# Second mixture: the first expert's plain results weighed inside the additions of the second expert, and one slot product moved by two slots

## The chip, the core and the metric

One core of a Trainium2 chip runs the whole program as a single launch. The metric is the time of one execution on the device, in microseconds (us). Five engines share the work: TensorE (PE in the profile, its weight loads PEld), VectorE (DVE), ScalarE (ACT), GpSimd (POOL) and SyncE (SP), which here issues the transfers.

## The reference, cut to what matters

Three layers follow each other: an attention with a memory term, a mixture of experts over slots, and a second mixture. Only the third is touched. It gets x (2304 rows, 512 columns) and eight experts with weights of 512 x 1024 and 1024 x 512:

```python
logits = x @ w_gate
P = np.exp(logits - logits.max())
for _ in range(8):
    P /= P.sum(1, keepdims=True) + 1e-09
    P /= P.sum(0, keepdims=True) + 1e-09
    P *= N / E
for e in range(E):
    out += P[:, e:e+1] * (np.maximum(x @ w1[e], 0.0) @ w2[e])
```

The eight rounds on P are called the balancing below. P is not known before they have ended.

## The kernel before, in words

**The grid.** The second mixture is a list of 72 units: eight experts times nine row blocks `u` of 256 rows, expert by expert. Unit 0 is expert 0 with u = 0, unit 9 is expert 1 with u = 0, and so on. A unit multiplies hidden values (256 x 1024) with one expert's second weights (1024 x 512) and adds the result to accumulators that stay in SBUF: `accA`, `accB` and `accD`, which hold the four 128 x 256 blocks of each row block and one intermediate sum.

**Two kinds of units.** Units 0 to 5 (`RAW = 6`) run while the balancing is still under way. They multiply plainly (`plain`, L1336) and `store` their result unweighed on ScalarE. From unit 6 on, P is known and lies already in the hidden values, and a unit uses seven block products instead of eight (`product`, L1369 to L1371), in the order p5, p1, p7, p6, p2, p3, p4. Each product ends in PSUM, and `collect` adds it to an accumulator: on ScalarE as a copy where the accumulator is new (L1383), on VectorE as an addition otherwise (L1385).

**Slots.** A unit has seven slots, and slot s = 7 * unit + k. In each slot the engines' instruction lists get one product, or seven plain matmuls, and the side steps that a table `side` holds for that slot, in the order in which they were entered. The order on TensorE, VectorE, ScalarE and GpSimd is exactly that of the code.

**Preparing the next unit.** While a unit multiplies, its successor's hidden values are made. `layer1` (L1052) is TensorE's first layer for the next unit, in slot 1 of a product unit: eight matmuls into two PSUM banks. `hidden` then spreads work over slots 2 to 6 and slot 0 of the next unit: ScalarE takes relu and the high parts (L1072, L1082), VectorE sums and low parts out of PSUM (L1076, L1089), GpSimd the low parts of the sums (L1093). The last one on VectorE is `a22l` (L1089). After it the two banks are free for the next `layer1`.

**Side steps.** The next expert's weights are summed (`w_sum`, L960) and split into high and low parts (`w_hi` on ScalarE, L963, `w_lo` mostly on GpSimd, L969). For expert 1 the steps of T1, T2 and T4 stand in slots 29 to 51. `scale_c`, `turn_c` and `store_c` put P into the small matrix that `layer1` reads, in units 6 to 10 for expert 1 and in the same place of each later expert. `prepare_a` (L999) multiplies the slots with an expert's first weights into the one PSUM bank `aux`, `split_a` splits that (L1008, L1010), and `move_a` has SyncE copy it to its place. `sum_columns` (L1203, tile `pcs`) uses the same bank `aux` between `balance_rows` (L1189 to L1197) and `balance_columns` (L1207 to L1210), in slots 9 + 3n, 10 + 3n and 11 + 3n.

**Settling.** Units 0 to 5 left their results unweighed, so `settle` (L1279) multiplies the four blocks of row block u by column 0 of P, one 128 x 256 block per slot, in slots 3 to 6 of unit 6 + u. That is 24 instructions on VectorE, in units 6 to 11.

Of the kernel before, what the change touches and what calls it, by code (L numbers as in the profile page):

```python
# [12 lines left out]
ALU = mybir.AluOpType  # L13
# [8 lines left out]
def infini_attention_soft_moe_sinkhorn_moe(  # L22
# [15 lines left out]
    nc = tc.nc  # L38
# [73 lines left out]
    with ExitStack() as actx:  # L112
        def pool(nm, bufs=1):
# [13 lines left out]
            out=maskw[:, 3 * P :], in_=maskw[:, 3 * P :], compare_op=ALU.is_ge,  # L127
# [6 lines left out]
        for j in range(2):  # L134
            sl = maskt[64 * j : 64 * j + 64]
            nc.gpsimd.affine_select(
                out=sl, in_=sl, compare_op=ALU.is_ge,
# [6 lines left out]
        for i in range(QTB):  # L144
            pr = []
            for nm, w in (("qz", 3 * TAIL), ("qx", 2 * TAIL)):
                t = e2.tile([P, w], F32R, name=f"{nm}{i}")
# [5 lines left out]
        for i in range(2):  # L153
            t = ep[i].tile([P, 2, S], F32R, name=f"klz{i}")
# [75 lines left out]
        for c0, c1 in ((0, 2 * P), (2 * P, S)):  # L230
# [14 lines left out]
            out=gB[:, 1, :], in0=gB[:, 0, :], scalar1=-1.0, scalar2=1.0,  # L245
            op0=ALU.mult, op1=ALU.add,
# [427 lines left out]
        def at(p, n, f, *args):  # L674

            fill.setdefault(3 * NT * p + n, []).append((f, args))
# [84 lines left out]
    with bctx:  # L761
# [57 lines left out]
        for g in range(E // 4):  # L819
# [3 lines left out]
            for n in range(FF // 512):  # L823
# [3 lines left out]
                for c in range(KD):  # L827
                    for j in range(4):
                        e = SPE * (4 * g + j)
# [54 lines left out]
    CW = DM // 2  # L884
# [4 lines left out]
    RAW = 6  # L889
# [77 lines left out]
    def w_lo(e, nm, i, g):  # L967
# [12 lines left out]
        out=sel.rearrange("p j c -> p (j c)"), in0=ones[:, 0:1].to_broadcast([P, 640]),  # L980
        scalar1=0.0, scalar2=None, op0=ALU.mult,
# [59 lines left out]
    accA = mB.tile([P, NU, DM], F32, name="accA")  # L1041
    accB = mB.tile([P, NU, DM], F32, name="accB")
    accD = mB.tile([P, NU, CW], F32, name="accD")
# [83 lines left out]
    Pr = mB.tile([P, NTT, E], F32, name="Pr")  # L1127
# [120 lines left out]
    def beside(s, f, *args):  # L1248
        side.setdefault(s, []).append((f, args))
# [11 lines left out]
    def both(t):  # L1261
        return t.rearrange("p (o c) -> p o c", o=1).to_broadcast([P, 2, CW])

    def halves(t):
        return t.rearrange("p (o c) -> p o c", o=2)

    def add_u(u, g):

        A, B_, D_ = accA[:, u], accB[:, u], accD[:, u]
        eng(g[0]).tensor_tensor(  # L1270
            out=halves(B_), in0=halves(B_), in1=both(A[:, 0:CW]), op=ALU.add
        )
        eng(g[1]).tensor_tensor(out=D_, in0=D_, in1=A[:, 0:CW], op=ALU.add)

    def settle(u, i):

        A, B_, D_ = accA[:, u], accB[:, u], accD[:, u]
        t, T = ((A[:, CW:], 0), (B_[:, 0:CW], 0), (B_[:, CW:], 1), (D_, 1))[i]
        nc.vector.tensor_scalar(  # L1279
            out=t, in0=t, scalar1=Pr[:, 2 * u + T, 0:1], scalar2=None, op0=ALU.mult  # L1280
        )

    def at(u, k, f, *args):
        beside(7 * u + k, f, *args)

    def c_steps(v, e, u0, u1):
        at(v, 1, scale_c, e, u0, u1)
        at(v, 2, turn_c, e, u0, u1)
        at(v, 3, store_c, e, u0, u1)
# [15 lines left out]
    for e in range(1, E):  # L1305
        v = NU * (e - 1)
        for i in range(5):
            c_steps(v + 6 + i, e, 2 * i, min(2 * i + 2, NU))
        at(v, 0, load_w1, e, e % 2)
        at(v + 3 * (e == 1), 4, load_raw, e)  # L1310
        at(v + 1, 3, prepare_a, e)
        at(v + 1, 4, split_a, e)
        at(v + 1, 5, move_a, e)
        for i in range(2):
            for n, nm in enumerate(("T1", "T2", "T4")):

                s = 29 + 4 * (3 * i + n) if e == 1 else 7 * (v + 2 + 3 * i + n) + 1
                beside(s, w_sum, e, nm, i, "P")
                beside(s + 2 - (e == 1), w_hi, e, nm, i)
                beside(s + 3 - (e == 1), w_lo, e, nm, i, "P")  # L1320
            at(v + 6 + i, 2, w_sum, e, "T3", i, "P")
        for nm, k in (("B11", 2), ("T3", 4), ("B21", 6), ("B22", 8)):
            for i in range(2):
                at(v + 8, k + i, w_hi, e, nm, i)
                at(v + 8, k + i + (nm[0] == "B" and nm[1] == "2"), w_lo, e, nm, i, "D" if nm == "B22" and i else "P")
    for u in range(RAW):
        for i in range(4):
            at(6 + u, 3 + i, settle, u, i)


    def plain(g, k):
# [42 lines left out]
    def collect(g, k, y):  # L1374
        e, u = units[g]
        nm = ORDER[k]

        A, B_, D_ = accA[:, u], accB[:, u], accD[:, u]
        new, end = e == 0, e == E - 1

        def put(acc, y, new=new):
            if new:
                nc.scalar.activation(out=acc, in_=y, func=AF.Copy)  # L1383
            else:
                nc.vector.tensor_tensor(out=acc, in0=acc, in1=y, op=ALU.add)  # L1385

        def send(i, c, t):
            r0 = P * (2 * u + i)
            nc.sync.dma_start(out[r0 : r0 + P, CW * c : CW * c + CW], t)

        if nm == "p5":
            put(halves(B_), both(y))
        elif nm == "p1" and e == 1 and u < RAW:
            put(A[:, 0:CW], y, True)
            put(A[:, CW:], y)
        elif nm == "p1":
            put(halves(A), both(y))
        elif nm == "p7":
            put(D_, y)
        elif nm == "p2":  # L1400
            put(A, Y[g, "y3"], False)
            if end:
                send(0, 0, A[:, CW:])
                if u == NU - 1:
                    add_u(u, "DP")
        elif nm == "p3":
            put(B_, Y[g, "y2"], False)
            if end and u == NU - 1:
                send(0, 1, B_[:, 0:CW])
                send(1, 1, B_[:, CW:])  # L1410
        elif nm == "p4":
            put(D_, y, False)
            if end:
                if u < NU - 1:
                    add_u(u, "PP")
                    send(0, 1, B_[:, 0:CW])
                    send(1, 1, B_[:, CW:])
                send(1, 0, D_)
# [6 lines left out]
    def result(s):  # L1425
        if s in EX:
            collect(*EX.pop(s))
# [117 lines left out]
```

## Time and profile before

| | |
|---|---|
| median of 3 runs | 1150.27 us (1144.68 to 1154.06) |
| the profiled execution, its own time | 1150.16 us |
| its span, first to last instruction | 1148.4 us |
| TensorE busy | 1093.7 us, 95% |
| VectorE busy | 873.3 us, 76% |
| ScalarE / GpSimd busy | 640.9 / 659.4 us |
| plain units 0 to 5 | about 324 to 409 us of the span |
| units 6 to 11, with settling | about 409 to 490 us |

The profiled execution lies 0.11 us under the median. The span leaves out 1.8 us around the first and last instruction. TensorE is busy nearly all the time, so what matters are the few places where it is not.

### The profile page before, as it was taken

Reading aid. Unit: us, or ns where it says so; the run is one execution under the profiler, and the core shown is the slowest. Engines: PE = TensorE matmul, PEld = TensorE weight load, DVE = VectorE, ACT = ScalarE, POOL = GpSimd, SP = SyncE. Lnnn points to the kernel's source line nnn. Section 1 sums busy time; section 2 is a strip of 40 time slices with the busy share of each in tenths; the row PEclk is TensorE's granted clock in tenths of the full one; section 3 lists DMA queues with packets and bytes.
Section 4 is the critical chain, followed back from the end, with each engine's and each line's share of the span. In section 5 each row is a group of like instructions: output and inputs, shape, how many; then the busy total and the mean of one; then the engine's idle time right before and its main releaser. Section 6 shows DMA issues by size and latency. Waiting matters only on the chain.

```text
span 1148.4 us, 24410 instructions
## 1 busy us (share of the span) xinstructions
PE 1093.7 (95%) x9191; PEld 990.3 (86%) x9191; DVE 873.3 (76%) x1894; ACT 640.9 (56%) x1385; POOL 659.4 (57%) x602
## 2 busy tenths in 40 slices
PE   5899999998999999999999999999999999999998
PEld 4677777773377888899999999999999999999998
DVE  6788888875036568878778877877887887788876
ACT  6888878761233366455645644555464565456542
POOL 5333333300324287568767867786885777678665
PEclk9999999997989999999999999999999999999999
DMA  6677777338922003100400320130031013000111
GB/s 162 191 207 221 204 220 203 92 108 359 372 74 92 1 2 129 38 1 4 145 20 1 111 56 1 37 116 16 1 132 35 1 45 112 11 2 3 54 56 56
DMA packets 42789, 106.01 MB, mean 92 GB/s; under 512 B 8240, under 2 KB 18608, under 8 KB 38576
## 3 DMA queue, kind: packets, MB, share of 16 engines
q1 hardware_dynamic: 42240, 104.37, 28.4%
q8 instruction: 73, 1.20, 0.4%
q14 instruction: 44, 0.36, 0.1%
q10 hardware_dynamic: 432, 0.09, 0.0%
HBM read 96.04 MB, written 4.72 MB: 88 GB/s over the span
## 4 chain that ended last, share of the span: by engine, by line
PE 76%; DVE 14%; ACT 6%; issue 2%; DMA 1%; POOL 0%; SPq 0%; DVEq 0%; ACTq 0%
PE y L1369 16%; PE y L1371 16%; PE y L1370 16%; PE y L1336 5%; PE l L1052 5%; PE po L436 3%; DVE f L1076 2%; PE ph L830 2%; ACT sm L360 2%; PE pt L399 2%; PE pa L999 1%; PE pso L848 1%; DVE sm L356 1%; PE pc L1236 1%; PE pma L449 1%
## 5 line engine op out<-in xcount | busy, mean ns | idle before, releaser
L1076 DVE SCALAR_TENSOR_TENSOR f<-l,f 128x512 f32<-128x512 f32 x264 | 181.3, 687 | 57.4 <-ACT a11h L1082 49.4
L1093 POOL TENSOR_TENSOR s1l<-f,s1h 128x512 fp32r<-128x512 f32 x66 | 88.6, 1342 | 153.3 <-ACT s1h L1082 149.3
L1385 DVE TENSOR_TENSOR accA<-accA,y 128x512 f32<-128x512 f32 (+1 forms) x129 | 86.6, 671 | 41.1 <-PE y L1371 37.6
L1082 ACT ACTIVATE a12h<-l 128x512 fp32r<-128x512 f32 x72 | 43.3, 601 | 98.6 <-PE y L1371 82.3
L1093 POOL TENSOR_TENSOR s4l<-f,s4h 128x512 fp32r<-128x512 f32 x66 | 86.2, 1306 | 19.6 <-PE y L1370 10.4
L1385 DVE TENSOR_TENSOR accB<-accB,y 128x512 f32<-128x512 f32 x129 | 88.3, 685 | 5.0
L1093 POOL TENSOR_TENSOR s3l<-f,s3h 128x512 fp32r<-128x512 f32 x66 | 86.0, 1303 | 2.0 <-ACT s3h L1082 2.0
L1052 PE MATMUL l<-c4T,a 128*128 128x256 f32 x576 | 80.0, 282 | 6.9 <-DVE a22l L1089 6.0
L1093 POOL TENSOR_TENSOR s2l<-f,s2h 128x512 fp32r<-128x512 f32 x66 | 86.2, 1307 | 0.0
L360 ACT ACTIVATE sm<-sm,mn 128x128 f32<-128x128 f32 (+3 forms) x128 | 71.1, 556 | 19.6 <-DVE mn L356 17.9
L1052 PEld LDWEIGHTS l<-c4T,a 128*128 128x128 f32 x576 | 72.5, 190 | 9.9 <-DVE a22l L1089 8.3
L1072 ACT ACTIVATE f<-l 128x512 f32<-128x512 f32 x66 | 39.0, 592 | 72.8 <-PE l L1052 71.9
L1369 PE MATMUL y<-T2h,s2h 128*128 128x256 f32 x264 | 76.4, 289 | 0.0
L1369 PE MATMUL y<-T1h,s1h 128*128 128x256 f32 x264 | 73.4, 278 | 1.5 <-DVE accA L1385 1.5
L1369 PE MATMUL y<-BB1h,a11h 128*128 128x256 f32 x264 | 73.4, 278 | 1.1 <-DVE accB L1385 1.1
L969 POOL TENSOR_TENSOR BB1l<-raw,BB1h 128x512 fp32r<-128x512 f32 x32 | 41.1, 1300 | 57.8 <-ACT BB1h L963 53.6
L1370 PE MATMUL y<-BB2l,s4h 128*128 128x256 f32 x264 | 73.5, 278 | 0.4 <-DVE BB2l L969 0.3
L1369 PE MATMUL y<-BB2h,a12h 128*128 128x256 f32 x264 | 73.7, 279 | 0.0
L1371 PE MATMUL y<-BB1h,s3l 128*128 128x256 f32 x264 | 73.3, 278 | 0.1
L1370 PE MATMUL y<-T2l,s2h 128*128 128x256 f32 x264 | 73.3, 278 | 0.0
L1371 PE MATMUL y<-T2h,s2l 128*128 128x256 f32 x264 | 73.2, 277 | 0.0
L1371 PE MATMUL y<-BB1h,a11l 128*128 128x256 f32 x264 | 73.1, 277 | 0.0
(314 smaller groups left out, 4221.7 us busy)
## 6 DMA issues: line engine op xcount, KB each, us to landing
wm<-in_moe_w_dram SPq DMA_DIRECT2D x32, 1024.0 KB, 8.1
raw<-in_moe_w_dram SPq DMA_DIRECT2D x32, 512.0 KB, 3.9
w<-in_moe_w_dram SPq DMA_DIRECT2D x32, 512.0 KB, 4.3
qd<-in_q_dram SPq DMA_DIRECT2D x30, 288.0 KB, 4.3
kd<-in_k_dram SPq DMA_DIRECT2D x30, 288.0 KB, 4.5
qp<-in_q_dram SPq DMA_DIRECT2D x16, 288.0 KB, 3.6
vt<-in_v_dram SPq DMA_DIRECT2D x16, 256.0 KB, 2.8
out_dram<-accB SPq DMA_DIRECT2D x18, 128.0 KB, 1.8
```

The lines of the kernel that those rows point to most:

```text
L360: nc.scalar.activation(out=sm[:, 0:n], in_=sm[:, 0:n], func=AF.Exp, scale=-1.0, bias=mnc, accum_out=X.sums[:, i, h : h + 1],)
L969: eng(g).tensor_tensor(out=w_tile(e, nm, "l")[:, h], in0=full(e, nm, i), in1=w_tile(e, nm, "h")[:, h].bitcast(F32), op=ALU.subtract,)
L1052: nc.tensor.matmul(ph[:, f, :], a4s[e][:, P * (KH * j + f) : P * (KH * j + f) + P], c4T[:, UT * u : UT * u + UT], start=True, stop=True,)
L1072: nc.scalar.activation(out=f_tile(g, nm), in_=ph(g, nm), func=AF.Relu)
L1076: nc.vector.scalar_tensor_tensor(out=f_tile(g, nm), in0=ph(g, src), scalar=0.0, in1=b, op0=ALU.max, op1=op)
L1082: nc.scalar.activation(out=h_tile(g, nm, "h"), in_=ph(g, nm) if a else FU[g, nm], func=AF.Relu if a else AF.Copy)
L1093: nc.gpsimd.tensor_tensor(out=lo, in0=FU[g, nm], in1=hi, op=ALU.subtract)
L1336: nc.tensor.matmul(Y[g, i], X[g, f"a{i}{j}", "hhl"[n]][:, f, :], BB[j, "hlh"[n]][:, f].rearrange("p a c -> p (a c)"), start=j == 1 and f = ...
L1369: nc.tensor.matmul(o_, hh[:, f, :], wh[:, f, :], start=f == 0, stop=False)
L1370: nc.tensor.matmul(o_, hh[:, f, :], wl[:, f, :], start=False, stop=False)
L1371: nc.tensor.matmul(o_, hl[:, f, :], wh[:, f, :], start=False, stop=f == KH - 1)
L1385: nc.vector.tensor_tensor(out=acc, in0=acc, in1=y, op=ALU.add)
```

## The change

`settle` and its 24 instructions are taken out. The multiplication moves into `collect` of units 9 to 14 (expert 1, u = 0 to 5), the first that add to the unweighed blocks. There a new helper `weigh` computes accumulator times P plus product in one instruction, a scalar_tensor_tensor on VectorE. The product p5, which goes to both halves of `accB`, was one 128 x 512 addition and becomes two 128 x 256 instructions, since the halves have different columns of P. The additions of p1 (its second target) and p7 keep their size.

Separately, for expert 1 alone, `prepare_a` moves from slot 10 to slot 12, `split_a` from 11 to 12 and `move_a` from 12 to 13. Slot 10 is where the first `sum_columns` stands.

```diff
-    def settle(u, i):
-
-        A, B_, D_ = accA[:, u], accB[:, u], accD[:, u]
-        t, T = ((A[:, CW:], 0), (B_[:, 0:CW], 0), (B_[:, CW:], 1), (D_, 1))[i]
-        nc.vector.tensor_scalar(
-            out=t, in0=t, scalar1=Pr[:, 2 * u + T, 0:1], scalar2=None, op0=ALU.mult
-        )
...
-        at(v + 1, 3, prepare_a, e)
-        at(v + 1, 4, split_a, e)
-        at(v + 1, 5, move_a, e)
+
+        at(v + 1, 3 + 2 * (e == 1), prepare_a, e)
+        at(v + 1, 4 + (e == 1), split_a, e)
+        at(v + 1, 5 + (e == 1), move_a, e)
...
-    for u in range(RAW):
-        for i in range(4):
-            at(6 + u, 3 + i, settle, u, i)
...
+        def weigh(acc, T):
+
+            nc.vector.scalar_tensor_tensor(
+                out=acc, in0=acc, scalar=Pr[:, 2 * u + T, 0:1], in1=y, op0=ALU.mult, op1=ALU.add
+            )
...
-        if nm == "p5":
+        plain_before = e == 1 and u < RAW
+        if nm == "p5" and plain_before:
+            weigh(B_[:, 0:CW], 0)
+            weigh(B_[:, CW:], 1)
+        elif nm == "p5":
             put(halves(B_), both(y))
-        elif nm == "p1" and e == 1 and u < RAW:
+        elif nm == "p1" and plain_before:
             put(A[:, 0:CW], y, True)
-            put(A[:, CW:], y)
+            weigh(A[:, CW:], 0)
+        elif nm == "p7" and plain_before:
+            weigh(D_, 1)
```

**On VectorE in unit 7**, between the first sums (`f`) for unit 8 and its last low part (`a22l`), this stood before; the four rows at L1279 are the settling:

```order
L1076 SCALAR_TENSOR_TENSOR f<-l_5270,f 128x512 x2
L1279 TENSOR_SCALAR accA<-accA,Pr 128x256
L1076 SCALAR_TENSOR_TENSOR f<-l_5265,f 128x512
L1089 SCALAR_TENSOR_TENSOR a11l<-l_5270,a11h 128x512
L1279 TENSOR_SCALAR accB<-accB,Pr 128x256
L1385 TENSOR_TENSOR accA<-accA,y_5311 128x512
L1076 SCALAR_TENSOR_TENSOR f<-l_5265,f 128x512
L1279 TENSOR_SCALAR accB<-accB,Pr 128x256
L1385 TENSOR_TENSOR accB<-accB,y_5284 128x512
L1089 SCALAR_TENSOR_TENSOR a12l<-l_5265,a12h 128x512
L1279 TENSOR_SCALAR accD<-accD,Pr 128x256
L1385 TENSOR_TENSOR accD<-accD,y_5374 128x256
```

The same stretch now (L1375 is the addition that was L1385):

```order
L1076 SCALAR_TENSOR_TENSOR f<-l_5266,f 128x512 x2
L1076 SCALAR_TENSOR_TENSOR f<-l_5261,f 128x512
L1089 SCALAR_TENSOR_TENSOR a11l<-l_5266,a11h 128x512
L1375 TENSOR_TENSOR accA<-accA,y_5307 128x512
L1076 SCALAR_TENSOR_TENSOR f<-l_5261,f 128x512
L1375 TENSOR_TENSOR accB<-accB,y_5280 128x512
L1089 SCALAR_TENSOR_TENSOR a12l<-l_5261,a12h 128x512
L1375 TENSOR_TENSOR accD<-accD,y_5367 128x256
```

Four rows are gone, and nothing else moved. **On VectorE in unit 9**, the first unit of expert 1, this stood before at the head of the unit:

```order
L1089 SCALAR_TENSOR_TENSOR a22l<-l_5428,a22h 128x512
L1385 TENSOR_TENSOR accB<-accB,y_5564 128x512
L1221 TENSOR_TENSOR cP<-Cw,Pr 128x128
L1231 TENSOR_TENSOR c_5622<-cP,chi 128x4x64
L1385 TENSOR_TENSOR accA<-accA,y_5594 128x256
L1076 SCALAR_TENSOR_TENSOR f<-l_5612,f 128x512 x2
L1385 TENSOR_TENSOR accD<-accD,y_5627 128x256
```

and now (L1379 is `weigh`):

```order
L1089 SCALAR_TENSOR_TENSOR a22l<-l_5420,a22h 128x512
L1379 SCALAR_TENSOR_TENSOR accB<-accB,Pr,y_5552 128x256 x2
L1221 TENSOR_TENSOR cP<-Cw,Pr 128x128
L1231 TENSOR_TENSOR c_5611<-cP,chi 128x4x64
L1379 SCALAR_TENSOR_TENSOR accA<-accA,Pr,y_5582 128x256
L1076 SCALAR_TENSOR_TENSOR f<-l_5600,f 128x512 x2
L1379 SCALAR_TENSOR_TENSOR accD<-accD,Pr,y_5616 128x256
```

Three additions became four weighing instructions in the same places. **On VectorE in unit 1**, where the first two rounds of the balancing meet the moved step (`alo` is the low part that `split_a` takes from the bank `aux`), before:

```order
L1210 TENSOR_TENSOR Pr<-Pr,cs 128x144
L1010 TENSOR_TENSOR alo<-pa,ahi 128x256
L1089 SCALAR_TENSOR_TENSOR a21l<-l_4484,a21h 128x512
L1189 TENSOR_REDUCE rr<-Pr 128x18
L1190 TENSOR_SCALAR rr<-rr 128x18
L1191 RECIPROCAL rr<-rr 128x18
L1192 TENSOR_TENSOR Pr<-Pr,rr 128x144
L1197 TENSOR_REDUCE cs<-Pr 128x8
```

and now:

```order
L1210 TENSOR_TENSOR Pr<-Pr,cs 128x144
L1089 SCALAR_TENSOR_TENSOR a21l<-l_4484,a21h 128x512
L1189 TENSOR_REDUCE rr<-Pr 128x18
L1190 TENSOR_SCALAR rr<-rr 128x18
L1191 RECIPROCAL rr<-rr 128x18
L1192 TENSOR_TENSOR Pr<-Pr,rr 128x144
L1197 TENSOR_REDUCE cs<-Pr 128x8
L1010 TENSOR_TENSOR alo<-pa,ahi 128x256
```

`alo` stands behind the second `balance_rows` now. On TensorE the 16 matmuls of `prepare_a` stood right behind the first `sum_columns` and stand now behind 14 further plain matmuls, with seven more before the second `sum_columns`. On ScalarE `ahi` changes places with `a21h`. The lists of GpSimd and SyncE keep their order.

## Rows read from the trace of the kernel before

**Rows 1.** The page, busy time of each engine.
```profile
PE 1093.7 (95%) x9191; PEld 990.3 (86%) x9191; DVE 873.3 (76%) x1894; ACT 640.9 (56%) x1385; POOL 659.4 (57%) x602
```

**Rows 2.** Two stretches: length; busy us of PE, PEld, DVE, ACT, POOL; clock; DMA.
```profile
412.22:502.51 90.29, 81.71 (x694) 78.16 (x695) 77.18 (x119) 48.72 (x97) 63.28 (x50) 1.00 0.16 54
523.36:601.68 78.32, 78.32 (x696) 77.09 (x695) 62.83 (x103) 43.81 (x84) 57.64 (x46) 1.00 0.19 62
```

**Rows 3.** Timeline of TensorE: layer1 in units 6 to 8, 15 and 16.
```profile
412.22 1.20 PE L1052 MATMUL l<-c4T,a 128*128 128x256 f32 x8 [0.60 <-DVE a22l L1089]
426.46 1.21 PE L1052 MATMUL l<-c4T,a 128*128 128x256 f32 x8 [1.19 <-DVE a22l L1089]
438.94 1.20 PE L1052 MATMUL l<-c4T,a 128*128 128x256 f32 x8 [1.13 <-DVE a22l L1089]
...
523.36 1.07 PE L1052 MATMUL l<-c4T,a 128*128 128x256 f32 x8
534.55 1.11 PE L1052 MATMUL l<-c4T,a 128*128 128x256 f32 x8
```

**Rows 4.** Chain of waits, 426.4 to 439.0 us: start, us, what.
```profile
427.61 0.52 ACT T4h L963
...
429.69 0.70 DVE f L1076
...
431.18 1.39 DVE accA L1279
...
433.70 0.34 DVE accB L1279
...
435.23 0.26 DVE accB L1279
...
436.69 1.27 DVE accD L1279
...
438.29 0.60 DVE a22l L1089
```

**Rows 5.** Groups on VectorE, 400 to 500 us, shapes kept apart.
```profile
L1279 DVE TENSOR_SCALAR accB<-accB,Pr 128x256 f32<-128x256 f32 x12 | 10.2, 847 | 0.0
L1279 DVE TENSOR_SCALAR accD<-accD,Pr 128x256 f32<-128x256 f32 x6 | 7.2, 1194 | 0.0
L1279 DVE TENSOR_SCALAR accA<-accA,Pr 128x256 f32<-128x256 f32 x6 | 7.1, 1185 | 0.0
...
L1385 DVE TENSOR_TENSOR accB<-accB,y 128x512 f32<-128x512 f32 x11 | 7.4, 676 | 0.1
...
L1231 DVE TENSOR_TENSOR c<-cP,chi 128x256 f32<-128x256 f32 x4 | 2.8, 710 | 1.7 <-ACT chi L1226 1.7
```

**Rows 6.** Two lines by themselves: durations min/median/max in ns.
```profile
L1279 DVE TENSOR_SCALAR accB<-accB,Pr x12: 335/640/1449, 419.0 to 488.2; 128x256 f32<-128x256 f32 x12
L1385 DVE TENSOR_TENSOR accD<-accD,y x129: 407/411/422, 425.4 to 1145.2; 128x256 f32<-128x256 f32 x129
```

**Rows 7.** Timeline of GpSimd from the end of unit 5 to unit 7.
```profile
407.39 2.55 POOL L969 TENSOR_TENSOR BB1l<-accB,BB1h 128x512 fp32r<-128x512 f32 x2
...
425.28 1.32 POOL L960 TENSOR_TENSOR ft<-raw,ft 128x512 f32<-128x512 f32 x1
...
436.52 1.29 POOL L1093 TENSOR_TENSOR s4l<-f,s4h 128x512 fp32r<-128x512 f32 x1 [1.31 <-ACT s4h L1082]
```

**Rows 8.** Timeline of ScalarE in unit 6.
```profile
420.27 0.63 ACT L963 ACTIVATE T2h<-ft 128x512 fp32r<-128x512 f32 x1 [1.10 <-POOL ft L960]
```

**Rows 9.** Timeline of TensorE: the first product of units 7 and 16.
```profile
421.04 0.38 PE L1369 MATMUL y<-T1h,s1h 128*128 128x256 f32 x1
...
531.73 0.28 PE L1369 MATMUL y<-T1h,s1h 128*128 128x256 f32 x1
```

**Rows 10.** Timeline of TensorE in units 1 and 2.
```profile
349.98 1.93 PE L999 MATMUL pa<-w,soT 128*32 128x256 f32 x32 [1.42 <-DVE cs L1207]
...
362.54 0.39 PE L1203 MATMUL pcs<-cs,ones 128*128 128x8 f32 x2 [0.66 <-DVE cs L1197]
```

## The prediction

> **What bounds the kernel now.** I first read the busy times: TensorE 1093.7 us, 95% of the span, VectorE 76% [rows 1]. That says that TensorE is the bound on the whole, and that a change on VectorE pays only where TensorE stands still. So I asked next where that is. The table by stretches answers it: seven units from 412.22 us on take 90.29 us with TensorE busy for 81.71, while the same seven places of the next expert, nine units later, take 78.32 us with TensorE busy all the time [rows 2]. The two stretches have the same products, the same `scale_c` steps and one `prepare_a`. The first is 11.97 us longer, at a granted clock of 1.00 in both.
>
> The timeline of TensorE names who is late: `layer1` waits 1.19 and 1.13 us for `a22l` on VectorE in units 7 and 8, and in units 15 and 16 it waits for nothing [rows 3]. The chain of waits through unit 7 then shows what makes `a22l` late. From 429.69 to 438.89 us it stays on VectorE, instruction behind instruction, and four links of it are settling: 1.39 + 0.34 + 0.26 + 1.27 = 3.26 us [rows 4]. So in units 6 to 11 VectorE is the bound, and from unit 13 on it is TensorE.
>
> **Part 1, settling goes.** It is 24 instructions with 10.2 + 7.2 + 7.1 = 24.5 us of VectorE's time [rows 5], 4.08 us per unit and 1.02 us each. On `accB` the shortest takes 0.335 us and the longest 1.449 [rows 6]; the one that the chain shows from 436.69 us for 1.27 ends 0.15 us behind a GpSimd operation that ran from 436.52 for 1.29 [rows 4, 7]. Taking 24.5 us away does not give 24.5: TensorE becomes the bound first. The ceiling is the difference of the two stretches, 11.97 us [rows 2]. Not all of it belongs to settling. From `layer1` of unit 6 to the first product of unit 7 it is 421.04 - 412.22 = 8.82 us, nine units later 531.73 - 523.36 = 8.37 [rows 3, 9]. VectorE has barely begun to settle there, so I leave these 0.45 us where they are. Gain: 11.97 - 0.45 = **11.5 us**. Bounds: nothing, if something else holds the units, and 11.97.
>
> The Trainium skill speaks against this term. VectorE: DVE Perf Modes, section "The perf-mode tier table", gives a one-source fp32 operation inside SBUF two elements per cycle, and an operation with a PSUM operand one. With that page's 150 fixed cycles, a settling instruction is (150 + 128) / 0.96 GHz = 0.29 us by my estimate, 7.0 us for 24, and the trade would be narrow work for wide work. No settling instruction here is that short, and the mean of the rows is three times as much, so by the measurement 24.5 us go.
>
> **Part 2, weighing comes.** The trace of before has no instruction of this form. Nearest from below is the plain addition of the same shape with one operand from PSUM: 407 to 422 ns over 129 instructions, median 411, whatever GpSimd did beside it [rows 6]. From above it is the longest settling instruction, 1.449 us [rows 6], which also reads an accumulator and a column of P. I take 0.411, because shape, the operand in PSUM and the accumulator are those of the addition. Per unit, four weighings take 4 x 0.411 = 1.64 us, and the additions that they replace 0.68 + 2 x 0.411 = 1.50 [rows 5, 6]: 0.14 us more, 0.8 in all of units 9 to 14. VectorE is idle for 78.32 - 62.83 = 15.5 us in seven such units [rows 2], 2.2 per unit, which hides it. Nobody waits long behind the split addition of p5 either: `a22l` stands ahead of it. Cost: 0.
>
> How much more could be hidden? Settling put 4.08 us per unit on VectorE and the six units grew by 11.5 / 6 = 1.92. So 4.08 - 1.92 = 2.16 us per unit were free, which fits the 2.2.
>
> **Part 3, the moved slot product.** `prepare_a` of expert 1 waited 1.42 us on TensorE, because the bank that it writes still held the column sums that VectorE had not read [rows 10]. In its new place 14 plain matmuls stand between the two, and the bank has long been read. The next taker of the bank, the second `sum_columns`, now waits for `alo`, which stands behind the second `balance_rows`. Seven plain matmuls cover that, and the sum itself could only be made after `balance_rows` anyway. Another such sum waited 0.66 us [rows 10], so the bounds are 1.42 - 0.66 = 0.76 and 1.42, and I take 1.4 because the cover is there. `move_a` and its 16 small transfers come one slot later on SyncE, in the same order; the `layer1` in unit 8 at 438.94 us [rows 3] first needs what they bring, over 80 us on. Gain: **1.4 us**.
>
> **Sum.** 11.5 + 1.4 - 0 = 12.9 us. The profiled execution took 1150.16 us (span 1148.4), and the median of the runs is 1150.27, so the profile stands for them: 1150.16 - 12.9 = **1137.3 us**.
>
> **The rivals.**
>
> *GpSimd takes the place of VectorE in units 6 and 7.* It works without a pause from 407.39 to 426.6 us [rows 7], and ScalarE already waits 1.10 us for it before `T2h` [rows 8], with the high parts for unit 7 queued behind that. From the end of `T2h` at 420.9 us, `a12h`, `a12l`, `a22h` and `a22l` of some 0.6 us each [rows 4] end at 423.3; `layer1` could start at 421.04 + (534.55 - 531.73) = 423.86 [rows 3, 9]. In unit 7 `T4h` needs the sum that ends at 426.6; from `T4h` to the end of `a22l` the chain took 438.89 - 427.61 = 11.28 us, 8.0 without settling [rows 4], which gives 434.6 against 423.86 + 11.19 = 435.05. Some 0.5 us to spare in both units: room, but little. If it is missed wholly, unit 7's `layer1` stays at 426.46 and unit 8's at 438.94: unit 6 keeps 14.24 us against 11.65, unit 7 keeps 12.48 against 11.19 [rows 3], 3.9 us together. Time 1141.2. Chance 0.17.
>
> *The weighings are held up as settling was.* They read the accumulator and a column of P from SBUF while GpSimd works, and the additions of two SBUF tensors at L1231, 0.71 us in the mean, show that VectorE can be slowed outside settling too [rows 5]. At settling's mean of 1.02 us, a unit gets 4.08 - 1.50 = 2.58 us more, 0.42 above what is free, times six units 2.5. Time 1139.8. Against it stands the addition with a PSUM operand, never held in 129 [rows 6]. SBUF — State Buffer of the Trainium skill, section "Who interferes with whom", says that a VectorE instruction with two SBUF inputs contends with a GpSimd one that reads SBUF, and that one with a single SBUF input does not; whether the column of P counts as an input it does not say. Chance 0.12.
>
> *Slower: every weighing starts just behind a GpSimd operation.* Then each waits about 1.3 us [rows 7] and takes 1.3 + 0.41 = 1.71. A unit gets 6.84 - 1.50 = 5.34 us, 3.18 over what is free, 19.1 us in units 9 to 14, more than the 12.9 gained: 1156.4. It decides from 4w - 1.50 - 2.16 = 12.9 / 6, so from w = 1.45 us per weighing, which only the longest settling instructions reached. Chance 0.03.
>
> *Settling is not what holds the units.* Then something else keeps `a22l` late, and only the moved product pays: 1148.8. It would be so if settling fitted into what VectorE has free. By the figures of VectorE: DVE Perf Modes in the Trainium skill, named above, it would fit: an estimated 1.16 us per unit. The chain, with 3.26 us of settling on it in one unit, speaks against it [rows 4]. That the change does not do what it says is in here too, though the order shows the 24 instructions gone. Chance 0.05.
>
> **How the numbers follow.** The forecast has the remaining 0.63, and its own range is 1133.5 to 1141: executions of one kernel lie several us apart (1144.68 to 1154.06 here), and the terms are sure to perhaps 1.5. The range for 8 in 10 takes in the two rivals at 1141.2 and 1139.8 and the same scatter: **1132.5 to 1144**. A measurement of this kernel tells about 1% from no change, here 11.5 us, so faster begins below 1138.8. The forecast lies close to that line: some 0.77 of it falls below, 0.485, and a little of the held weighings, 0.035: faster 0.52. Slower by over 1% needs 1161.8, beyond every case priced, and I leave 0.03 for what I did not see. No change: 0.45.
>
> **What would show it.** In the profile after: no L1279; 24 instructions at L1379 of about 0.41 us; `layer1` in units 7 to 12 without waits for `a22l` and some 11.2 us apart in units 7 to 9, as between 523.36 and 534.55; TensorE busy throughout the stretch of seven units, which then takes about 78.8 us; `prepare_a` of expert 1 without the 1.42 us. I am wrong if a wait of like size stands elsewhere: `T2h` or `T4h` with ScalarE idle behind GpSimd and `a22l` late behind them, weighings near 1 us, or a second `sum_columns` that waits for `alo`.

## The result, and the profile after

The changed kernel took 1138.78 us in the median, against 1149.85 us for the kernel before: ratio 0.9901, 95% interval 0.9875 to 0.9927. The forecast was 1137.3 us, the range 1132.5 to 1144. One of its six executions ran with TensorE at a granted clock of 0.76 and took 1341 us: it counts in that median, which is 1137.70 us without it, but not in the ratio, and since it was the profiled one, all rows of after are those of a later execution of the same kernel that took 1138.72 us.

In a second round of measuring, the same kernel had a median of 1143.09 against 1149.45: ratio 0.9947, interval 0.9922 to 0.9971, single executions from 1138.47 to 1154.52 us. The two intervals overlap by little. What may stand behind that scatter is told at the end; here it means that a per cent is near the limit of what the times tell, and that the terms of the sum have to be read from the profile.

The page of after, busy time of each engine as in [rows 1]:

```profile
span 1136.6 us, 24388 instructions
PE 1090.2 (96%) x9191; PEld 987.0 (87%) x9191; DVE 854.5 (75%) x1876; ACT 640.1 (56%) x1385; POOL 658.5 (58%) x602
```

VectorE is busy for 18.8 us less, not 24.5. The 24 weighings take 11.4 us, 2.5 more than the additions that they replaced; the other 3.2 us are not broken down here. TensorE has the same 9191 matmuls. Next the two stretches of seven units, in the columns of [rows 2]; the first runs from `layer1` of unit 6 to that of unit 13, the second over the same places of the next expert:

```profile
408.60:489.37 80.77, 78.84 (x695) 77.07 (x695) 58.22 (x100) 48.62 (x97) 62.74 (x50) 1.00 0.18 60
510.22:588.25 78.03, 78.00 (x696) 76.49 (x695) 63.24 (x103) 43.78 (x84) 57.60 (x46) 1.00 0.19 62
```

The first stretch fell from 90.29 to 80.77 us, by 9.52. It is still 2.7 us longer than its neighbour, and TensorE still stands for 1.9 us in it. `layer1` in TensorE's timeline, to be held against [rows 3]:

```profile
408.60 1.19 PE L1052 MATMUL l<-c4T,a 128*128 128x256 f32 x8 [0.60 <-DVE a22l L1089]
420.04 1.07 PE L1052 MATMUL l<-c4T,a 128*128 128x256 f32 x8
432.71 1.11 PE L1052 MATMUL l<-c4T,a 128*128 128x256 f32 x8
443.69 1.07 PE L1052 MATMUL l<-c4T,a 128*128 128x256 f32 x8
455.14 1.20 PE L1052 MATMUL l<-c4T,a 128*128 128x256 f32 x8 [0.17 <-DVE a22l L1089]
```

The waits of 1.19 and 1.13 us in units 7 and 8 are gone. The distances are 11.44, 12.67, 10.98 and 11.45 us: unit 7 is the odd one. What it waits for shows in the timelines of TensorE, then of ScalarE:

```profile
426.95 0.38 PE L1359 MATMUL y<-BB2h,s4h 128*128 128x256 f32 x1 [1.22 <-ACT accD L1373]
```

```profile
416.59 0.64 ACT L963 ACTIVATE T2h<-ft 128x512 fp32r<-128x512 f32 x1 [2.05 <-POOL ft L960]
...
423.08 0.63 ACT L963 ACTIVATE T4h<-ft 128x512 fp32r<-128x512 f32 x1 [1.75 <-POOL ft L960]
423.62 0.58 ACT L1373 ACTIVATE accA<-y 128x512 f32<-128x512 f32 x1
...
426.54 0.36 ACT L1373 ACTIVATE accD<-y 128x256 f32<-128x256 f32 x1
```

The product p3 writes into the other half of the PSUM bank that holds p7, and waits until p7 is copied out. That copy, to `accD`, stands on ScalarE behind `T4h`, which waited 1.75 us for a sum on GpSimd. In unit 10 it is `prepare_a` that waits for ScalarE, behind the copy of `store_c`:

```profile
459.73 0.64 PE L999 MATMUL pa<-w,soT 128*32 128x256 f32 x8 [0.39 <-ACT c4T L1241]
```

The weighing instructions, in the form of [rows 6]:

```profile
L1379 DVE SCALAR_TENSOR_TENSOR accB<-accB,Pr,y x12: 472/475/481, 443.1 to 499.0; 128x256 f32<-128x256 f32 x12
L1379 DVE SCALAR_TENSOR_TENSOR accA<-accA,Pr,y x6: 480/481/481, 445.9 to 500.4; 128x256 f32<-128x256 f32 x6
L1379 DVE SCALAR_TENSOR_TENSOR accD<-accD,Pr,y x6: 470/472/473, 448.4 to 503.1; 128x256 f32<-128x256 f32 x6
```

Minimum, median and maximum lie within 11 ns: none of the 24 was held up. GpSimd was at work beside most of them: for 12 all the time, and they took 473 to 481 ns, for 7 not at all, and they took 472 to 481. And the moved slot product, as in [rows 10]:

```profile
349.61 1.93 PE L999 MATMUL pa<-w,soT 128*32 128x256 f32 x32
352.98 0.28 PE L1203 MATMUL pcs<-cs,ones 128*128 128x8 f32 x2
358.91 0.39 PE L1203 MATMUL pcs<-cs,ones 128*128 128x8 f32 x2 [0.66 <-DVE cs L1197]
```

The wait of 1.42 us before it is gone, the second column sum waits for nothing, and the third waits 0.66 us as before. From `layer1` of unit 1 to that of unit 2 it is 15.75 us now, and was 17.14.

**Where the time went between the two profiles.** The span fell by 11.8 us. Read from the starts of `layer1`: 0.3 up to unit 0, 1.9 in unit 0, 1.4 in unit 1, nothing from there to unit 6, 9.5 in the seven units, and 1.3 given back after unit 13, where the slower pace of TensorE that is described at the end costs 3.2 us in this execution and 1.9 in the one before. The 1.9 us in unit 0 are not of the change's making. The granted clock there was 0.72 in the execution before and 1.00 in this one, as the row of this stretch shows, first for before, then for after:

```profile
318.00:330.00 12.00, 10.13 (x47) 9.07 (x48) 4.83 (x12) 4.38 (x10) 0.00 (x0) 0.72 0.48 175
```

```profile
318.00:330.00 12.00, 9.83 (x57) 8.08 (x58) 4.57 (x10) 4.70 (x10) 1.30 (x1) 1.00 0.48 175
```

### The profile page after: what moved, and what is told of

It reads as the page before. It is cut to its first block, busy times and chain, and to the rows that moved or that the text cites. A ratio compares the mean times of both kernels' runs of the same rounds, so it can differ in the third digit from the quotient of the medians.

```text
span 1339.0 us, 24388 instructions
## 1 busy us (share of the span) xinstructions
PE 1310.9 (98%) x9191; PEld 1173.5 (88%) x9191; DVE 850.6 (64%) x1876; ACT 648.9 (48%) x1385; POOL 657.2 (49%) x602
## 4 chain that ended last, share of the span: by engine, by line
PE 96%; DVE 1%; ACT 1%; issue 0%; POOL 0%; DMA 0%; SPq 0%; DVEq 0%; ACTq 0%; POOLq 0%
PE y L1359 19%; PE y L1361 19%; PE y L1360 19%; PE y L1326 6%; PE l L1052 6%; PE po L436 4%; PE pt L399 3%; PE ph L830 2%; PE ps L354 2%; PE ps L355 2%; PE pso L848 1%; PE pa L999 1%; PE pc L1236 1%; PE pma L449 1%; PE ps L340 1%; PE ps L335 1%
## 5 line engine op out<-in xcount | busy, mean ns | idle before, releaser
L1375 DVE TENSOR_TENSOR accA<-accA,y 128x512 f32<-128x512 f32 x123 | 84.4, 686 | 112.1 <-PE y L1361 112.1
L1375 DVE TENSOR_TENSOR accB<-accB,y 128x512 f32<-128x512 f32 x123 | 84.5, 687 | 50.2 <-PE y L1361 49.7
L1052 PE MATMUL l<-c4T,a 128*128 128x256 f32 x576 | 93.2, 313 | 0.9 <-DVE a L66 0.9
L1093 POOL TENSOR_TENSOR s2l<-f,s2h 128x512 fp32r<-128x512 f32 x66 | 85.4, 1295 | 11.1 <-ACT s2h L1082 10.3
L1052 PEld LDWEIGHTS l<-c4T,a 128*128 128x128 f32 x576 | 86.9, 221 | 2.3 <-DVE a L66 1.1
L1359 PE MATMUL y<-T2h,s2h 128*128 128x256 f32 x264 | 86.0, 326 | 0.0
L1360 PE MATMUL y<-T4l,a22h 128*128 128x256 f32 x264 | 82.4, 312 | 0.0
L1361 PE MATMUL y<-T4h,a22l 128*128 128x256 f32 x264 | 82.3, 312 | 0.0
L1361 PE MATMUL y<-T1h,s1l 128*128 128x256 f32 x264 | 82.3, 312 | 0.0
L1359 PE MATMUL y<-BB1h,s3h 128*128 128x256 f32 x264 | 82.3, 312 | 0.0
L1360 PE MATMUL y<-T1l,s1h 128*128 128x256 f32 x264 | 82.3, 312 | 0.0
L1360 PE MATMUL y<-BB1l,s3h 128*128 128x256 f32 x264 | 82.1, 311 | 0.0
```

The costliest lines, as they stand in the source:

```text
L1052: nc.tensor.matmul(ph[:, f, :], a4s[e][:, P * (KH * j + f) : P * (KH * j + f) + P], c4T[:, UT * u : UT * u + UT], start=True, stop=True,)
L1093: nc.gpsimd.tensor_tensor(out=lo, in0=FU[g, nm], in1=hi, op=ALU.subtract)
L1359: nc.tensor.matmul(o_, hh[:, f, :], wh[:, f, :], start=f == 0, stop=False)
L1360: nc.tensor.matmul(o_, hh[:, f, :], wl[:, f, :], start=False, stop=False)
L1361: nc.tensor.matmul(o_, hl[:, f, :], wh[:, f, :], start=False, stop=f == KH - 1)
```

## The experiments

All are compared with the kernel before, run beside them: medians 1149.45 us (first four), 1151.28 (next four) and 1150.64 (last four). "The seven units" is always the stretch from `layer1` of unit 6 to that of unit 13: 90.29 us before, 80.77 after.

**The changed kernel again.** No edit.

> The changed kernel once more, for an undisturbed profile. Theory (VectorE's settling held units 6 to 11, TensorE takes over): 1137 to 1139 us; layer1 in units 7 to 12 without a wait for a22l, the seven units from layer1 of unit 6 to that of unit 13 in 78.8 us (90.29 before), 24 weighings of about 0.41 us, prepare_a of expert 1 without its 1.42 us. Rival (GpSimd takes VectorE's place in units 6 and 7): a22l late in those two units, the stretch 80 to 83 us. Rival (weighings held up by GpSimd): their mean near 1 us.

1143.09 us, ratio 0.9947 (0.9922 to 0.9971), above the 1137 to 1139 that were expected; the profile is the one above. `prepare_a` came as the theory has it, the weighings took 0.475 us instead of 0.41, and the stretch of 80.77 us did not come: it lies at the foot of what the GpSimd rival gives, but through another instruction than `a22l`.

**Weighing alone.**

```diff
-        at(v + 1, 3 + 2 * (e == 1), prepare_a, e)
+        at(v + 1, 3, prepare_a, e)
```

(and `split_a`, `move_a` likewise)

> Settling replaced by weighing, prepare_a left in slot 10. Theory: the gain of part 1 alone, 11.5 us, so about 1138.5 against 1149.9, and in the profile prepare_a of expert 1 still waits about 1.4 us. Rival (the moved product carries more than its own wait): 1141 or more.

1138.67 us, ratio 0.9901 (0.9882 to 0.9920), five executions from 1137.77 to 1139.48. The seven units take 80.79 us, and `prepare_a` waits as it did:

```profile
348.42 1.93 PE L999 MATMUL pa<-w,soT 128*32 128x256 f32 x32 [1.43 <-DVE cs L1207]
```

So part 1 alone brings 9.5 us in the profile, whatever the slot product does.

**The move alone.**

```diff
-        at(v + 1, 3, prepare_a, e)
+        at(v + 1, 3 + 2 * (e == 1), prepare_a, e)
```

(and `split_a`, `move_a` likewise, in the kernel before)

> prepare_a of expert 1 moved to slot 12, settling left as before. Theory: 1.4 us less than before, 1148.5, which the times alone will hardly show; in the profile the wait of 1.42 us before prepare_a is gone and the second sum_columns waits less than 0.7 us. Rival (the wait is given back at the next column sum): the second sum_columns waits 1 us or more, and 1149.9.

1149.93 us, ratio 0.9994 (0.9977 to 1.0012). The times show nothing, as expected. In the profile the wait is gone:

```profile
351.82 1.93 PE L999 MATMUL pa<-w,soT 128*32 128x256 f32 x32
355.18 0.28 PE L1203 MATMUL pcs<-cs,ones 128*128 128x8 f32 x2
```

and unit 1 takes 15.78 us instead of 17.14. The term of 1.4 us is real, and too small for the times to see.

**Half the settling.** In the changed kernel, `settle` is back for the two blocks of `accB`, and p5 is a plain addition again.

```diff
+    for u in range(RAW):
+        for i in (1, 2):
+            at(6 + u, 3 + i, settle, u, i)
...
-        if nm == "p5" and plain_before:
-            weigh(B_[:, 0:CW], 0)
-            weigh(B_[:, CW:], 1)
-        elif nm == "p5":
+        if nm == "p5":
```

> The changed kernel with the two blocks of accB settled as before (12 of the 24 instructions, 10.2 of their 24.5 us, 1.7 us per unit) and the other two weighed. Theory (VectorE has about 2.16 us free per unit, only what goes beyond costs time): no loss against the changed kernel, 1138 to 1139. Rival (each us of settling costs in proportion, 11.5/24.5): 10.2 x 0.47 = 4.8 us lost, 1143 to 1144.

1142.36 us, ratio 0.9938 (0.9916 to 0.9960). That is above the theory's 1138 to 1139 and just below the rival's 1143 to 1144; but since the changed kernel itself had 1143.09 in this round and 1138.78 in the first, the times do not decide. The profile does. The seven units take 84.37 us, 3.6 more than 80.77:

```profile
408.69:493.06 84.37, 81.20 (x694) 77.72 (x695) 67.83 (x107) 48.68 (x97) 62.89 (x50) 1.00 0.18 57
```

Of the 3.6 us, 2.0 fall into unit 9, 0.9 into unit 11 and 0.6 into unit 6; units 7 and 8 lose 0.1 and nothing. Settling was 12.0 us here, 2.0 per unit, below the 2.16 that I took for free. So there is no such sum that holds for every unit: in units 7 and 8 two us cost nothing, in unit 9, where VectorE also splits a piece of the weights (`BB2l`, 1.1 us here), they cost 2.0. The theory falls in this strong form. The rival's 4.8 us lie closer to the 3.6 in sum, but they do not fall in proportion on the units either.

**Later T3 sums, with the move and without.** Two sums for expert 1 on GpSimd move from slots 44 and 51 to 53 and 55, the later part of unit 7.

```diff
-            at(v + 6 + i, 2, w_sum, e, "T3", i, "P")
+            at(v + 6 + i + (e == 1 and i == 0), 2 + 2 * (1 + i) * (e == 1), w_sum, e, "T3", i, "P")
```

> The changed kernel with the two T3 sums of expert 1 moved later on GpSimd, from slots 44 and 51 to 53 and 55. In the changed kernel's undisturbed profile the third-last product of unit 7 waits 1.22 us for a copy on ScalarE that stands behind T4h, which waits 1.75 us for GpSimd. Theory (GpSimd is the chain behind that wait, one sum too many ahead of it): the wait is gone, unit 7 takes 11.4 us instead of 12.67, the seven units 79.5 us instead of 80.77; 1.3 us in time, too little for the times alone. Rival (ScalarE's own order is the limit): the wait stays near 1.2 us.

> The same, with prepare_a of expert 1 left in slot 10. It repeats beside the run above the comparison of a moved with an unmoved slot product, which came out as 1143.1 against 1138.7 us. Theory (the move saves 1.4 us and costs nothing; the higher median came from a slower pace of TensorE that falls on some experts in some executions): within 3 us of the run above, and 1.4 us above it by the intervals of the profile. Rival (the move itself costs about 4 us): 3 to 5 us below the run above.

1139.08 us, ratio 0.9912 (0.9886 to 0.9937) with the move, and 1140.45 us, 0.9903 (0.9884 to 0.9923) without. The wait of 1.22 us is gone, and unit 7 takes 11.30 us instead of 12.67. With the order of ScalarE the same, GpSimd is shown to be behind that wait. But unit 9 now takes 12.62 us instead of 11.45: TensorE stands there several times for a short while, for 0.30 us before a product that needs a low part from GpSimd, which has to do the moved work later, and for 0.26 us before a `turn_c`.

```profile
446.30 0.39 PE L1361 MATMUL y<-BB1h,s3l 128*128 128x256 f32 x1 [0.30 <-POOL s3l L1093]
```

The seven units take 80.50 us, so nearly all of it is given back. Between the two runs there is no difference clear of the noise, and none between the move alone and the kernel before: that moving `prepare_a` costs 4 us, as the medians 1143.09 and 1138.67 of the changed kernel and of weighing alone suggested, is not borne out.

**Settling elsewhere.** Four multiplications by 1.0 per unit, in slots 3 to 6 of units 20 to 25 of the changed kernel.

```diff
+    def extra(u, i):
+        t = (accA[:, u, CW:], accB[:, u, 0:CW], accB[:, u, CW:], accD[:, u])[i]
+        nc.vector.tensor_scalar(out=t, in0=t, scalar1=ones[:, 0:1], scalar2=None, op0=ALU.mult)
...
+    for n in range(RAW):
+        for i in range(4):
+            at(20 + n, 3 + i, extra, (5 + n) % NU, i)
```

> The changed kernel with four instructions like settling per unit (a block of an accumulator times 1.0) on VectorE in slots 3 to 6 of units 20 to 25, 24 in all, far from the start of the product units. Theory (it was VectorE's load of 4 us per unit, not something about units 6 to 11): instructions of 0.34 to 1.45 us, about 1.9 us more per unit, 10 to 12 us in all, 1149 to 1151, and layer1 waits for a22l there. Rival (units 6 to 11 were long because expert 1's weights are made in a hurry there): under 4 us more.

1152.47 us, ratio 1.0013 (0.9996 to 1.0029): the whole gain is gone again. Units 20 to 25 take 12.27, 12.38, 12.38, 12.64, 13.79 and 13.82 us, instead of 10.43 four times, 10.88 and 11.10 in an expert without the extra work; that is 13.6 us more, and units 26 and 27 add 0.7. `layer1` there shows the picture of [rows 3] again:

```profile
580.56 1.19 PE L1052 MATMUL l<-c4T,a 128*128 128x256 f32 x8 [1.15 <-DVE a22l L1089]
592.94 1.20 PE L1052 MATMUL l<-c4T,a 128*128 128x256 f32 x8 [1.15 <-DVE a22l L1089]
```

So it was the load on VectorE, not the place. The instructions took 337 to 1456 ns, and GpSimd decides which:

```profile
L1278 DVE TENSOR_SCALAR accB<-accB,ones x12: 337/891/1456, 574.2 to 641.8; 128x256 f32<-128x256 f32 x12
L1278 DVE TENSOR_SCALAR accA<-accA,ones x6: 1151/1154/1164, 571.9 to 636.9; 128x256 f32<-128x256 f32 x6
L1278 DVE TENSOR_SCALAR accD<-accD,ones x6: 1345/1348/1350, 578.2 to 643.2; 128x256 f32<-128x256 f32 x6
```

```profile
587.84 1.33 POOL L1093 TENSOR_TENSOR s3l<-f,s3h 128x512 fp32r<-128x512 f32 x1
590.52 1.29 POOL L1093 TENSOR_TENSOR s4l<-f,s4h 128x512 fp32r<-128x512 f32 x1 [1.34 <-ACT s4h L1082]
...
589.15 0.34 DVE L1278 TENSOR_SCALAR accB<-accB,ones 128x256 f32<-128x256 f32 x1
590.61 1.35 DVE L1278 TENSOR_SCALAR accD<-accD,ones 128x256 f32<-128x256 f32 x1
```

The first of the two begins as `s3l` on GpSimd ends, and takes 0.34 us. The second begins while `s4l` runs and ends 0.15 us behind it. All 24 are of these two kinds: 18 end 146 to 152 ns behind the end of a GpSimd instruction, and the 6 short ones met no more than the last 28 ns of one.

**Sums in the same places.** The same 24 places and columns, with a reduction into one column. The diff is against the run above.

```diff
+    red = mS.tile([P, 1], F32, name="red")
...
-        nc.vector.tensor_scalar(out=t, in0=t, scalar1=ones[:, 0:1], scalar2=None, op0=ALU.mult)
+        nc.vector.tensor_reduce(out=red, in_=t, op=ALU.add, axis=AX.X)
```

> The same 24 places, each with a sum over the same 256 columns into one column instead of the multiplication, so as many instructions on as many elements. Theory (what cost time was that each instruction stood still beside GpSimd; a sum does not): about 0.4 us each whatever GpSimd does, 1.6 us per unit, under the 2.2 that VectorE has free, so within 2 us of the changed kernel. Rival (four more instructions per unit cost time by their number or their place in the chain): 5 us or more above it.

1151.71 us, ratio 1.0016 (0.9998 to 1.0034). By the times the rival had it. But units 20 to 23 took 10.74 or 10.75 us, and units 29 to 32, without any sums, 10.81, and all others of their kind 10.74 to 10.84: the whole program had become slower, from unit 11 to the end. The kernel differs in one more thing, the tile `red` of four bytes per partition. Two further runs separate the two.

**The sums without a new tile.** `red` is replaced by a column of the unused tile `gap` that is already there. The diff is against the run above.

```diff
-    mS.tile([P, 24], F32, name="gap")
+    gap = mS.tile([P, 24], F32, name="gap")
...
-    red = mS.tile([P, 1], F32, name="red")
...
-        nc.vector.tensor_reduce(out=red, in_=t, op=ALU.add, axis=AX.X)
+        nc.vector.tensor_reduce(out=gap[:, 0:1], in_=t, op=ALU.add, axis=AX.X)
```

> The 24 sums again, but written into a tile that is there anyway and unused, so that no tile changes its place in SBUF. The run before had one more tile of four bytes per partition, and every unit of the whole program took 10.74 to 10.84 us there instead of 10.43. Theory (the sums cost nothing, the changed places of the tiles cost the time): units 20 to 23 take 10.4 us, 1138 to 1143 us. Rival (the sums cost it): 1149 or more.

1139.85 us, ratio 0.9881 (0.9849 to 0.9913). Units 20 to 23 take 10.43 us with four sums in each:

```profile
572.58 1.07 PE L1052 MATMUL l<-c4T,a 128*128 128x256 f32 x8
583.01 1.07 PE L1052 MATMUL l<-c4T,a 128*128 128x256 f32 x8
593.43 1.07 PE L1052 MATMUL l<-c4T,a 128*128 128x256 f32 x8
```

```profile
L1278 DVE TENSOR_REDUCE gap<-accB x12: 408/410/411, 577.7 to 633.0; 128x1 f32<-128x256 f32 x12
```

Four instructions of 0.41 us in a unit cost nothing; four of 1.1 us in the mean, on the same columns in the same places, cost 1.8 to 2.9 us per unit. All 24 sums lie wholly beside a GpSimd instruction, and they took 407 to 413 ns. So what costs time is that the multiplications stand still beside GpSimd.

**The tile without the sums.** The changed kernel, with the tile alone.

```diff
+    mS.tile([P, 1], F32, name="red")
```

> The changed kernel with the additional tile of four bytes per partition alone, used by nothing. Theory (the places of the tiles that come behind it set TensorE's pace): 10.74 to 10.84 us in the units without other work throughout, 1149 to 1153 us. Rival (no instruction changes, so no time does): 1138 to 1143.

1152.76 us, ratio 1.0015 (0.9998 to 1.0032), with not one instruction more than the changed kernel. The same units now:

```profile
570.70 1.10 PE L1052 MATMUL l<-c4T,a 128*128 128x256 f32 x8
581.45 1.10 PE L1052 MATMUL l<-c4T,a 128*128 128x256 f32 x8
592.19 1.10 PE L1052 MATMUL l<-c4T,a 128*128 128x256 f32 x8
```

10.75 us each instead of 10.43, at a granted clock of 1.00. The four bytes cost 12.9 us, against 1139.85 for the kernel with the sums in `gap`, which ran beside it. Since no instruction differs, what is left are the places of the tiles that were allocated behind the new one.

**Earlier sums.** The steps of T1, T2 and T4 for expert 1 three slots apart.

```diff
-                s = 29 + 4 * (3 * i + n) if e == 1 else 7 * (v + 2 + 3 * i + n) + 1
+                s = 29 + 3 * (3 * i + n) if e == 1 else 7 * (v + 2 + 3 * i + n) + 1
```

> The changed kernel with the steps of expert 1's T1, T2 and T4 three slots apart instead of four, so that GpSimd has done them by slot 46 instead of 51; the T3 sums stay. Theory (GpSimd is late in units 6 and 7 because too much of expert 1's weights falls there, and has time in units 4 and 5): the wait of 1.22 us in unit 7 is gone and nothing comes in unit 9 for it, unlike with the later T3 sums: seven units in 78.5 to 79.6 us instead of 80.77, 1 to 2 us less in time. Rival (the work only collides elsewhere): 80.5 or more.

1143.01 us, ratio 0.9919 (0.9886 to 0.9951); the seven units take 81.16 us. The rival had it: unit 7 falls to 11.32 us, unit 9 stays at 11.42, but in unit 6 a product waits 1.79 us:

```profile
414.29 0.39 PE L1361 MATMUL y<-BB1h,s3l 128*128 128x256 f32 x1 [1.79 <-POOL s3l L1093]
```

**Settling on ScalarE.** In the kernel before, with `prepare_a` moved.

```diff
-        nc.vector.tensor_scalar(
-            out=t, in0=t, scalar1=Pr[:, 2 * u + T, 0:1], scalar2=None, op0=ALU.mult
-        )
+        nc.scalar.activation(out=t, in_=t, func=AF.Copy, scale=Pr[:, 2 * u + T, 0:1])
```

> Settling as in the kernel before, but on ScalarE (24 copies with a scale, some 0.36 us each, 1.45 us per unit), prepare_a moved as in the change. Theory (VectorE's load was what cost time; ScalarE is busy for 48.6 of 80.8 us there): the seven units in 80 to 83 us, 1139 to 1143. Rival (ScalarE stands in the chain to a22l too, and its order is full): 85 us or more, 1144 and above.

1141.82 us, ratio 0.9908 (0.9881 to 0.9935); the seven units take 82.62 us, of which 0.8 belong to the slower pace described at the end. The 24 copies took 0.50 us each rather than 0.36. Taking settling off VectorE brought most of the gain. That it vanished into the additions is worth about 1 us more in these profiles, 81.8 us without the slower pace against 80.8, which the times cannot show.

None of the versions beats the changed kernel clearly.

## Why the prediction was right

**The bound, right.** VectorE held units 6 to 11, and settling was what made it late. Shown from both sides: without settling, by fusing it or by putting it on ScalarE, the seven units fall to 80.8 and 82.6 us, and with as much settling in units 20 to 25 those grow by 13.6. It was held through more than `a22l`: in the kernel before, two products also waited for additions on VectorE.

```profile
423.59 0.39 PE L1369 MATMUL y<-BB1h,a11h 128*128 128x256 f32 x1 [0.93 <-DVE accB L1385]
462.07 0.36 PE L1369 MATMUL y<-T1h,s1h 128*128 128x256 f32 x1 [1.24 <-DVE accA L1385]
```

The one instruction that the prediction caught ending 0.15 us behind GpSimd stands for most: of the 24 of the kernel before, 17 end 148 to 156 ns behind the end of a GpSimd instruction, and the other 7 take 335 to 344 ns.

**Part 1, mis-sized: 11.5 foretold, 9.5 measured.** The step that failed is the one that took the stretch of the next expert, with 0.45 us on top, for what would remain: 78.8 us, and it was 80.77. The two stretches are alike for TensorE, but not for the engines that feed it: [rows 2] has GpSimd busy for 63.28 against 57.64 us and ScalarE for 48.72 against 43.81, and in the profile of after the same gap is left. I had the chain right that could prevent it, GpSimd to `T2h` and `T4h` on ScalarE, and gave it 0.17 as a rival. The sign that I had named came half: `T2h` and `T4h` stood behind GpSimd with ScalarE idle, 2.05 and 1.75 us. I followed the chain only to `a22l`, found 0.5 us to spare, and `a22l` was indeed in time in units 7 and 8. I did not ask what else stands behind `T4h` on ScalarE: the copy of p7 out of the bank that p3 needs. That is 1.22 us of wait in unit 7; the 0.39 us of `prepare_a` in unit 10 stand behind a copy on ScalarE, too. Against the neighbouring stretch in its own profile (10.89, 11.10, 10.88, 11.41, 12.90), units 6 to 10 lose 0.55, 1.57, 0.10, 0.04 and 0.47 us. Both attempts to take GpSimd's work out of the way moved the wait to another unit, which shows that GpSimd has little room from unit 6 to unit 9.

**Part 2, right in effect, low in size.** A weighing takes 0.475 us, not 0.411: 1.5 us more in all, hidden as foreseen. The rival that they would be held up is refuted by the 11 ns between the fastest and the slowest, with GpSimd and without. The prediction left open whether the column of P counts as a second SBUF input by the rule of SBUF — State Buffer in the Trainium skill, section "Who interferes with whom": by these 24 it does not. For a single SBUF input that rule has a condition that the prediction did not pass on: it speaks of instructions outside the modes that use both ports. The same section says that a reduction never contends with GpSimd; with 407 to 413 ns for 24 sums beside a busy GpSimd the trace of the sums in `gap` agrees.

**The estimate from a table.** By VectorE: DVE Perf Modes in the Trainium skill, section "The perf-mode tier table", a settling instruction would be an estimated 0.29 us, and by that figure taking it away would have brought nothing. The shortest took 0.335 us before and 0.337 in the experiment, near it. The mean was 1.02 us, and that mean is what cost time. So 24 instructions that can be done in 0.34 us were exchanged for 24 of 0.475, and it paid because the new ones do not stand still.

**Part 3, right.** 1.4 us: unit 1 takes 15.75 to 15.78 us in all ten profiles with the move and 17.14 to 17.17 in the three without it, and nothing is given back at the second column sum. The times alone do not show it.

**The free time of 2.16 us per unit, wrong as it was put.** It was an average over six units, and half the settling, 2.0 us per unit, already cost 3.6 us. It priced two rivals that did not come, so the forecast did not hang on it.

**The sum, in part luck.** The terms that belong to the change are worth 9.5 + 1.4 = 10.9 us in the profiles, against 12.9 foretold, and the medians of the first comparison differ by 11.1. The second comparison gave 6.4, the two kernels with later sums 12.2 and 10.8. That the time came within 1.5 us of the forecast says little for the terms: the medians of the same kernel in the two rounds lie 4.3 us apart, and the execution from which the forecast was reckoned held 1.9 us of a lowered clock in unit 0, which the profile of after does not have and the change did not remove; they are nearly the 2.0 us by which part 1 was missed. The chances of 0.52 and 0.45 for the two sides of one per cent fit a result that lies on that line in the first comparison, and on the side of no change in the second.

## What to carry to other kernels

Before taking work off the engine that is late, list for each in-order engine next to it everything that stands behind its own longest wait, not only the instruction that is late now: the next bound was one copy further down ScalarE's list. A short instruction that lasts three times its minimum is worth more to remove or to change in form than its element count says, and here a fused form with an operand in PSUM kept to 470 to 481 ns beside GpSimd and without it. When a change adds a tile, measure the tile alone, too.

## What the runs showed of the hardware that was not expected

**TensorE has two paces at the same granted clock.** At 1.00, consecutive matmuls of 256 columns start 113 ns apart in most units and 118 in others, which makes 10.43 or 10.84 us of a unit without other work, with its 92 matmuls. Two such units in the profile of after, from one `layer1` to the next:

```profile
577.83 1.07 PE L1052 MATMUL l<-c4T,a 128*128 128x256 f32 x8
588.25 1.07 PE L1052 MATMUL l<-c4T,a 128*128 128x256 f32 x8
...
1082.75 1.10 PE L1052 MATMUL l<-c4T,a 128*128 128x256 f32 x8
1093.58 1.11 PE L1052 MATMUL l<-c4T,a 128*128 128x256 f32 x8
```

The slower pace holds for four or five units in a row, mostly from a `prepare_a` to the next `turn_c`, and costs about 2 us each time, 3.2 where it lasts to the end, as in the profile of after. The number of such passages differs from execution to execution: one in the profile before and in that of after, three with the move alone and with settling on ScalarE, two with the sums in `gap`, one each with the later sums without the move and with the earlier ones, none in weighing alone, half the settling, the later sums with the move and settling elsewhere. With one profile per kernel it is not shown that the single times from 1138 to 1154 us are made of these, only that passages of this size exist and vary. What starts one is open.

**The place of tiles in SBUF sets a pace, too.** Four bytes per partition more in one pool, without any use, made units of 10.43 us into 10.74 to 10.84 throughout, 12.9 us in all. What it is about the places is open.

**A clock that falls before unit 1.** In some executions TensorE's granted clock was 0.72 in the mean from 318 to 330 us. In the profile of before it was at 0.50 in this stretch, the lower of its two levels of 1.2 and 2.4 GHz:

```profile
321.10:327.70 6.60, 6.60 (x24) 5.92 (x25) 2.60 (x6) 2.26 (x5) 0.00 (x0) 0.50 0.56 229
```

Unit 0 took 13.55 us there instead of 11.60. This was so in the profile before, with the move alone and with the earlier sums, for half as long with the sums in `gap` (13.15 us), and not in the other nine. What starts it is open: from 309 to 321 us, ahead of the fall, TensorE was busy for 8.97 us, and in the profile of after, where the clock stayed at 1.00, for 8.88. The 1.9 us are as much as the smaller terms of the prediction.
